# GEGLU feed-forward on one core: two feature tiles interleaved by product, and a head of two plain tiles with eight products taken ahead

## The chip, the cores and the metric

One core of one Trainium2 chip runs the whole program. The metric is the device time of one execution in microseconds (us), as a median of several executions. The profile shows one execution of each kernel; its span (first to last instruction) is about 1.8 us shorter than the device time of that execution.

Names used below: PE is TensorE (its matmuls), PEld its weight loads, DVE is VectorE, ACT is ScalarE, POOL is GpSimd, SP is the sync engine, which does nothing here but issue loads. "SPq" and "ACTq" are issues of loads on these two engines' queues. A load is issued at one time and "lands" when all its data is there. SBUF is the on-chip memory that tiles lie in, PSUM the banks that matmuls write to. KB is 1024 bytes. bf16 and fp32r are the 16-bit and the 32-bit float type of the matmuls here.

## The reference

```python
B, S, D, F = 32, 32, 1024, 3584        # bf16; x is 1024 x 1024 when flattened
def reference(x, w_gate, w_up, w_down):
    return (gelu(x @ w_gate) * (x @ w_up)) @ w_down
```

## The kernel before

The hidden layer has F/128 = 28 feature tiles. Four of them (the "head") are computed plainly: gate and up, for two token halves of 512, eight matmuls each. The other 24 tiles use a scheme with seven block products instead of eight (Strassen's, in Winograd's form): gate and up are two of the four blocks of one operand, the token halves the other. Five of the seven products are in fp32r, because their operands are sums; two are in bf16, because their operands are the inputs themselves. The down projection uses the same seven products once, on large blocks.

The head, cut to what matters (`plain` issues matmuls of a plain tile, `nb` is the token half):

```python
F0 = 4                                             # plain tiles
for q in range(1, 4):                              # loads: three more quarters of D
    load_xT(0, d0, d1)                             # x, transposed by the load, 256 KB
    load_w(nc.sync, 0, 0, d0, d1)                  # gate weights of the 4 tiles, 256 KB
    load_w(nc.sync, 0, 1, d0, d1)                  # up weights, 256 KB
load_xT(1, 0, KD); load_xT(1, KD, DT)              # second token half
...
for q in range(3):
    for which in (0, 1):                           # gate, up
        for dt in range(q * KQ, (q + 1) * KQ):
            for fl in range(F0):
                plain(head[fl][which], which, fl, 0, dt, dt + 1)
```

The loop takes one tile at a time. In it `prod` is four matmuls of 128x512:

```python
for ft in range(F0, FT):
    prod(psc, s1, t1, True)                 # fp32r
    sn5 = snap(psc, "sn5", 2)               # ACT copies PSUM to SBUF
    prod(psa, s2, t2, False)                # fp32r
    sn2 = snap(psa, "sn2", 1)
    if open_ft: last_product(open_ft)       # fp32r, of the tile before
    prod(psc, s4, b22r, False)              # fp32r
    c12 = added(sn2, psc)                   # DVE
    h1 = acc("G")                           # the gelu's result goes to a PSUM bank
    nc.scalar.activation(h1, c12, ACT.Gelu_apprx_tanh)
    prod(psb, quads(ci, fl)[1], b21, True)  # bf16: product P2
    ...
    ahead = first_product(ft + 1)           # bf16: product P1 of the next tile
    prod(psa, s3, t3, False)                # fp32r
    c22 = added(sn5, psa)
    tt(g_of(ft)[:, NB:], c22, h1, MUL)      # DVE
```

POOL makes the four weight sums s1 to s4 of the next two tiles meanwhile. PE's eight PSUM banks go by tags: A three, B two, C two, G one.

## Time and profile before

| | before |
|---|---|
| device time, median (3 runs at first) | 277.25 us |
| span of the profile | 275.2 us |
| PE busy | 270.1 us, 98% of the span |
| matmuls of 512 columns in the program | 432 bf16, 760 fp32r |

These lines are from the page of before: the span, then busy tenths in 40 equal slices (9 is 90% or more), PEclk is the granted clock of TensorE, and last the shares of the chain that ended last.

```profile
span 275.2 us, 3268 instructions
...
PE   8999999999999999999999999999999999999995
...
PEclk9999999999999999999999999999999999999999
...
PE 98%; issue 0%; ACT 0%
```

PE is full in every slice but the first and the last and makes up the whole chain: only fewer or cheaper matmuls, or fewer gaps between them, can shorten this kernel. The next lines are the timeline of PE for one tile of the loop (start in us, length in us, then line, tile written, tiles read, shapes, count).

```profile
56.21 1.03 PE L268 MATMUL psA<-b,wg 128*128 128x512 bf16 x4
56.88 1.27 PE L268 MATMUL psA<-t,s 128*128 128x512 f32 x4
...
60.72 1.07 PE L268 MATMUL psC<-b22r,s 128*128 128x512 f32 x4
61.86 0.81 PE L268 MATMUL psB<-b,wg 128*128 128x512 bf16 x3
62.51 0.38 PE L268 MATMUL psA<-b,wg 128*128 128x512 bf16 x1
```

From the start of one tile's P1 (56.21) to the next's (62.51) it is 6.30 us. The trace's start-to-start distances inside a run of equal matmuls are 216 ns for bf16 and 226 to 227 ns for fp32r. 8 x 216 + 20 x 226.7 ns are 6.26 us, so the two changes of type in each tile cost about 0.035 us together.

Of the head's loads, these are the three transposed ones of the first token half and the last up weights, as SP issues them (start, time that the issue takes):

```profile
1.74 1.33 SPq L189 DMA_TRANSPOSE b<-in_x_dram  x1
...
4.24 2.75 SPq L189 DMA_TRANSPOSE b<-in_x_dram  x1
...
8.18 1.27 SPq L189 DMA_TRANSPOSE b<-in_x_dram  x1
...
10.12 0.47 SPq L131 DMA_DIRECT2D wu<-in_w_up_dram  x1
```

PE's timeline from the first real matmul (4.38 us) to the start of the second token half (18.93 us):

```profile
4.38 1.39 PE L221 MATMUL psA<-b,wg 128*128 128x512 bf16 x3
...
6.48 0.38 PE L221 MATMUL psC<-b,wg 128*128 128x512 bf16 x1
6.84 0.60 PE L221 MATMUL psB<-b,wu 128*128 128x512 bf16 x2
...
15.91 0.59 PE L221 MATMUL psB<-b,wu 128*128 128x512 bf16 x2
...
18.93 1.89 PE L221 MATMUL psA<-b,wg 128*128 128x512 bf16 x8
```

In before, PE waits for loads only 0.14 us in this stretch (at the first up weights, 6.8 us). The last up weights of the first token half are issued at 10.12 us and land at 14.33 us.

### The profile page before, as it was taken

The numbers are of one execution on the slowest core, as the hardware profiler recorded it, in microseconds if no ns is written. First come the engines' busy times: TensorE is split into PE (matmuls) and PEld (weight loads), VectorE is DVE, ScalarE is ACT, GpSimd is POOL, SyncE is SP. The second block draws the span as 40 slices with busy tenths as digits, with TensorE's granted clock in tenths as the row PEclk, the third lists the DMA queues.
The fourth block names the chain that finished last, engine by engine and source line by source line (L and its number), as shares of the span: only waits on it lengthen the run. The fifth ranks groups of instructions, "written<-read, shape, count | busy, mean of one in ns | idle before, by whom it ended". The sixth has DMA issues, their size and how long they took to land.

```text
span 275.2 us, 3268 instructions
## 1 busy us (share of the span) xinstructions
PE 270.1 (98%) x1190; PEld 184.3 (67%) x1207; DVE 173.1 (63%) x184; ACT 114.4 (42%) x179; POOL 94.9 (34%) x51
## 2 busy tenths in 40 slices
PE   8999999999999999999999999999999999999995
PEld 3444467766677777777666777754447888888883
DVE  0049975555555555555555555556999999999511
ACT  4034455555555555555555555430200022972001
POOL 1000059996766749494947660000000000000000
PEclk9999999999999999999999999999999999999999
DMA  7999023150505143250508500003992245786202
GB/s 150 323 248 270 2 76 96 59 155 0 155 0 152 26 126 87 68 137 17 152 2 249 171 2 1 0 0 126 335 337 82 91 166 169 245 270 209 77 0 76
DMA packets 52192, 33.77 MB, mean 123 GB/s; under 512 B 8656, under 2 KB 52176, under 8 KB 52176
## 3 DMA queue, kind: packets, MB, share of 16 engines
q1 hardware_dynamic: 49184, 30.94, 39.1%
q10 hardware_dynamic: 2992, 2.62, 3.0%
q8 instruction: 9, 0.15, 0.2%
q14 instruction: 7, 0.06, 0.1%
HBM read 29.62 MB, written 2.10 MB: 115 GB/s over the span
## 4 chain that ended last, share of the span: by engine, by line
PE 98%; issue 0%; ACT 0%
PE psA L268 31%; PE psC L268 16%; PE psA L352 14%; PE psB L268 7%; PE psB L352 7%; PE psC L352 7%; PE psG L352 5%; PE psA L221 4%; PE psC L221 3%; PE psB L221 3%; PE psG L205 1%; PE psG L221 1%; PE tp L213 0%; ACT o_sb L491 0%; PE psG L217 0%
## 5 line engine op out<-in xcount | busy, mean ns | idle before, releaser
L268 PE MATMUL psA<-t,s 128*128 128x512 f32 x192 | 56.2, 414 | 0.0
L268 PEld LDWEIGHTS psA<-t,s 128*128 128x128 f32 x192 | 36.1, 188 | 9.4 <-ACT sn L279 0.2
L156 POOL TENSOR_TENSOR s<-wu 128x1024 fp32r<-128x1024 bf16 x11 | 23.7, 2150 | 29.3 <-PE psC L268 29.3
L284 DVE TENSOR_TENSOR c<-sn,psA 128x512 f32<-128x512 f32 x24 | 16.6, 690 | 25.4 <-PE psA L268 25.4
L268 PEld LDWEIGHTS <-wg 128*128 128x128 bf16 x192 | 16.9, 98 | 23.3 <-issue 6.3
L279 ACT COPY sn<-psA 128x512 f32<-128x512 f32 x48 | 27.8, 579 | 10.4 <-PE psA L268 10.4
L268 PE MATMUL psC<-t,s 128*128 128x512 f32 x96 | 26.1, 394 | 0.0
L268 PE MATMUL psA<-t,a22r 128*128 128x512 f32 x96 | 25.9, 391 | 0.0
L320 ACT ACTIVATE psG<-c 128x512 f32<-128x512 f32 x24 | 14.4, 602 | 27.4 <-DVE c L284 27.4
L268 PE MATMUL psC<-b22r,s 128*128 128x512 f32 x96 | 25.6, 389 | 0.0
L268 PE MATMUL psA<-b,wg 128*128 128x512 bf16 x96 | 24.6, 379 | 0.0
L158 POOL TENSOR_TENSOR s<-wg,s 128x1024 fp32r<-128x1024 bf16 x11 | 23.8, 2165 | 0.9
L157 POOL TENSOR_TENSOR s<-s,wg 128x1024 fp32r<-128x1024 f32 x11 | 23.5, 2137 | 0.9
L159 POOL TENSOR_TENSOR s<-wg,wu 128x1024 fp32r<-128x1024 bf16 x11 | 23.5, 2139 | 0.0
L268 PE MATMUL psB<-b,wg 128*128 128x512 bf16 x84 | 22.2, 381 | 0.8
L279 ACT COPY sn<-psC 128x512 f32<-128x512 f32 x24 | 14.1, 589 | 20.3 <-PE psC L268 20.3
L290 DVE TENSOR_TENSOR hi<-h,psA 128x512 bf16<-128x512 bf16 x14 | 9.6, 689 | 19.8 <-PE psA L268 19.8
L268 PEld LDWEIGHTS psC<-t,s 128*128 128x128 f32 x96 | 18.0, 188 | 4.3
L268 PEld LDWEIGHTS psA<-t,a22r 128*128 128x128 f32 x96 | 18.0, 188 | 3.8
L268 PEld LDWEIGHTS psC<-b22r,s 128*128 128x128 f32 x96 | 17.9, 188 | 3.8 <-ACT sn L279 0.2
L284 DVE TENSOR_TENSOR c<-sn,psC 128x512 f32<-128x512 f32 x24 | 16.5, 689 | 5.0 <-PE psC L268 5.0
L284 DVE TENSOR_TENSOR c<-sn,psB 128x512 f32<-128x512 f32 x24 | 16.5, 687 | 2.8
(99 smaller groups left out, 420.5 us busy)
## 6 DMA issues: line engine op xcount, KB each, us to landing
wg<-in_w_gate_dram SPq DMA_DIRECT2D x12, 512.0 KB, 4.0
wu<-in_w_up_dram SPq DMA_DIRECT2D x12, 512.0 KB, 5.2
wdb<-in_w_down_dram SPq DMA_DIRECT2D x12, 512.0 KB, 4.7
wdb<-in_w_down_dram SPq DMA_DIRECT2D x12, 384.0 KB, 4.2
v<-in_w_down_dram SPq DMA_DIRECT2D x4, 512.0 KB, 6.9
out_dram<-o_sb ACTq DMA_DIRECT2D x16, 128.0 KB, 1.7
v<-in_w_down_dram SPq DMA_DIRECT2D x4, 384.0 KB, 7.6
wg<-in_w_gate_dram SPq DMA_DIRECT2D x3, 256.0 KB, 3.9
```

What stands on the lines that cost most here:

```text
L156: yield eng.tensor_tensor(s1, a21, a22, ADD)
L157: yield eng.tensor_tensor(s2, s1, a11, SUB)
L158: yield eng.tensor_tensor(s4, a12, s2, SUB)
L159: yield eng.tensor_tensor(s3, a11, a21, SUB)
L205: nc.tensor.matmul(warm_ps, lhsT=ones_w, rhs=ones_m, start=True, stop=True)
L221: nc.tensor.matmul(ps, lhsT=w_tiles[0][which][:, dt, fl * P : (fl + 1) * P], rhs=x_rows(dt, nb), start=(dt == 0), stop=(dt == DT - 1),)
L268: nc.tensor.matmul(ps, lhsT=lhs[:, k, :], rhs=rhs[:, k, :], start=(start and k == 0), stop=(k == KD - 1), skip_group_check=True,)
L279: nc.scalar.copy(t, ps)
L284: tt(t, s, ps, ADD)
L290: tt(g_of(ft)[:, :NB], h0, psa, MUL)
L320: nc.scalar.activation(h1, c12, ACT.Gelu_apprx_tanh)
L352: nc.tensor.matmul(banks[m], lhsT=lhs(k)[:, m * P : (m + 1) * P], rhs=rhs(k), start=(start and k == 0), stop=(k == HF - 1), skip_group_che ...
```

## The change

The intent has three parts. First, 26 tiles instead of 24 in the form with seven products: 1184 matmuls instead of 1192. Secondly, the loop takes two tiles together and goes product by product, so that the four bf16 products of a pair stand in one block and the type changes half as often. Thirdly, the head with only two plain tiles has less work to cover its loads with, so the products P2 of the next eight tiles are computed in the head ("ahead") and kept in SBUF, in slots that later hold the hidden layer. The core of the diff:

```diff
-    F0 = 4
-    NCH = (FT - F0) // FC + 1
+    NCH = FT // FC
+    NAHEAD = 8
@@ banks
-        ... bufs={"A": 3, "B": 2, "C": 2, "G": 1}[tag]
+    BANKS = {"A": 4, "B": 2, "C": 2}
@@ loads of the head: the weight loads are half as large, and
+        load_ahead(0)                       # 512 KB for four ahead products
         load_xT(1, 0, KD)
         load_xT(1, KD, DT)
+        load_ahead(1)
@@ head
+        tok0 = [(acc("A"), acc("B")) for _ in range(FC)]
+        for q in range(3): ...              # as before, for two tiles
+        take_ahead(0, "CCAA", (nc.scalar.copy, nc.vector.tensor_copy) * 2)
+        ...                                 # second token half of the two tiles
+        take_ahead(1, "CCAA", (nc.scalar.copy,) * 4)
@@ loop
-        for ft in range(F0, FT):
+        for ci in range(1, NCH):
+            for fl in range(FC):
+                prod(psc[fl], s1[fl], t1, True)
+                sn5.append(snap(psc[fl], "sn5"))
+            for fl in range(FC):
+                prod(psa[fl], s2[fl], t2, False)
+                sn2.append(snap(psa[fl], "sn2"))
+            for st in open_fts:
+                last_product(st)
+            for fl, ft in enumerate(fts):
+                prod(psc[fl], s4[fl], b22r, False)
+                h1.append(gelu(added(sn2[fl], psc[fl]), "h1", 2))     # now in SBUF
+                a22r_of(ft)
+            if fts[0] < FC + NAHEAD:
+                h0 = first                                            # P2 was taken ahead
+            else:
+                ... # P2 of both tiles
+            begun = [first_product(ft + FC) for ft in fts]            # P1 of the next two
+            for fl, ft in enumerate(fts):
+                prod(psa[fl], s3[fl], t3, False)
+                tt(g_of(ft)[:, NB:], added(sn5[fl], psa[fl]), h1[fl], MUL)
```

The bank G is gone: the gelu result h1 goes to SBUF. The down projection does the same matmuls on renamed banks.

More of the change, by code (lines that the diff above doesn't have):

```diff
@@ L68 @@
     ring = ctx.enter_context(tc.tile_pool(name="ring", bufs=4))
-    opool = ctx.enter_context(tc.tile_pool(name="osb", bufs=4))
     one = ctx.enter_context(ExitStack())
@@ L101, in g_of @@
         return by_batch(g_lo if ft < HF else g_hi)(k)
+    BANKS = {"A": 4, "B": 2, "C": 2}
     def acc(tag):
-        return ps1.tile([P, NB], fp32, name=f"ps{tag}", tag=tag, bufs={"A": 3, "B": 2, "C": 2, "G": 1}[tag])
+        return ps1.tile([P, NB], fp32, name=f"ps{tag}", tag=tag, bufs=BANKS[tag])
+    a12_ahead = [ring.tile([P, KD, KB * P], bf16, name="a12a", tag="ring") for _ in range(NAHEAD // KB)]
     b11 = xpool.tile([P, KD, NB], bf16, name="b11")
@@ L114, in x_rows, with alloc_w, load_w_all @@
         return ((b11, b12), (b21, b22))[dt // KD][nb][:, dt % KD, :]
-    w_tiles = {
-        0: tuple(
-            gpool.tile([P, DT, F0 * P], bf16, name=n, tag=f"hi{KB}", bufs=2) for n in ("wg0", "wu0")
-        )
-    }
-    def alloc_w(ci):
-        w_tiles[ci] = tuple(
-            wpool.tile([P, DT, FC * P], bf16, name=n, tag=n, bufs=b) for n, b in (("wg", 3), ("wu", 2))
+    ahead = [
+        gpool.tile([P, KB, NB], fp32, name="ahead", tag=f"hi{KB}", bufs=2) for _ in range(NAHEAD // KB)
+    ]
+    w_tiles = {}
+    def alloc_w(ci, which):
+        w_tiles[ci, which] = wpool.tile(
+            [P, DT, FC * P], bf16, name=("wg", "wu")[which], tag=("wg", "wu")[which], bufs=(3, 2)[which]
         )
     def load_w(eng, ci, which, d0, d1):
-        f0, fc = (F0 + (ci - 1) * FC, FC) if ci else (0, F0)
+        f0 = ci * FC * P
         src = (wg_r, wu_r)[which]
-        eng.dma_start(out=w_tiles[ci][which][:, d0:d1, :], in_=src[:, d0:d1, f0 * P : (f0 + fc) * P])
-    def load_w_chunk(ci):
-        alloc_w(ci)
-        for which in (0, 1):
-            load_w(nc.sync, ci, which, 0, DT)
+        eng.dma_start(out=w_tiles[ci, which][:, d0:d1, :], in_=src[:, d0:d1, f0 : f0 + FC * P])
+    def load_w_all(ci, which):
+        alloc_w(ci, which)
+        load_w(nc.sync, ci, which, 0, DT)
     def quads(ci, fl=None):
         cols = slice(None) if fl is None else slice(fl * P, (fl + 1) * P)
-        wg, wu = w_tiles[ci]
+        wg, wu = w_tiles[ci, 0], w_tiles[ci, 1]
         return wg[:, :KD, cols], wg[:, KD:, cols], wu[:, :KD, cols], wu[:, KD:, cols]
-    def chunk_of(ft):
-        ci, fl = divmod(ft - F0, FC)
-        return ci + 1, fl
     s_tiles = {}
@@ L163, in a22r_of @@
     def a22r_of(ft):
-        t = spool.tile([P, KD, P], f32r, name="a22r", tag="a22r", bufs=3)
-        nc.scalar.copy(t, quads(*chunk_of(ft))[3])
+        t = spool.tile([P, KD, P], f32r, name="a22r", tag="a22r", bufs=2)
+        nc.scalar.copy(t, quads(*divmod(ft, FC))[3])
         a22rs[ft] = t
@@ L182 @@
             )
+        alloc_w(0, 0)
+        alloc_w(0, 1)
         for dt in range(KQ):
@@ L185, with load_ahead @@
         load_w(nc.scalar, 0, 1, 0, KQ)
+        def load_ahead(i):
+            f0 = (FC + i * KB) * P
+            nc.sync.dma_start(out=a12_ahead[i], in_=wg_r[:, KD:, f0 : f0 + KB * P])
         def load_xT(nb, d0, d1):
@@ L197 @@
             load_w(nc.sync, 0, 1, d0, d1)
+        load_ahead(0)
         load_xT(1, 0, KD)
         load_xT(1, KD, DT)
-        load_w_chunk(1)
-        load_w_chunk(2)
-        warm_ps = acc("G")
+        load_ahead(1)
+        load_w_all(1, 0)
+        load_w_all(1, 1)
+        load_w_all(2, 0)
+        warm_ps = acc("A")
         for _ in range(NWARM):
             nc.tensor.matmul(warm_ps, lhsT=ones_w, rhs=ones_m, start=True, stop=True)
-        tags = iter("CCAB")
+        tags = iter("CCBB")
         for dt in range(KQ):
@@ L210 @@
                 tag = next(tags)
-                tp = ps1.tile([P, hw], bf16, name="tp", tag=tag, bufs={"A": 3, "B": 2, "C": 2}[tag])
+                tp = ps1.tile([P, hw], bf16, name="tp", tag=tag, bufs=BANKS[tag])
                 for b in range(HALF):
@@ L222, in plain @@
                     ps,
-                    lhsT=w_tiles[0][which][:, dt, fl * P : (fl + 1) * P],
+                    lhsT=w_tiles[0, which][:, dt, fl * P : (fl + 1) * P],
                     rhs=x_rows(dt, nb),
@@ L227, in plain, with gelu @@
                 )
+        def gelu(src, tag, bufs):
+            h = ework.tile([P, NB], bf16, name=tag, tag=tag, bufs=bufs)
+            nc.scalar.activation(h, src, ACT.Gelu_apprx_tanh)
+            return h
         def plain_out(ft, nb, gate, up):
-            h = ework.tile([P, NB], bf16, name="h", tag="h")
-            nc.scalar.activation(h, gate, ACT.Gelu_apprx_tanh)
-            tt(g_of(ft)[:, nb * NB : (nb + 1) * NB], h, up, MUL)
-        head = [(acc(a), acc(b)) for a, b in ("AB", "AB", "AC", "CG")]
-        for q in range(3):
-            for which in (0, 1):
-                for dt in range(q * KQ, (q + 1) * KQ):
-                    for fl in range(F0):
-                        plain(head[fl][which], which, fl, 0, dt, dt + 1)
-        for fl in range(F0):
-            for which in (0, 1):
-                plain(head[fl][which], which, fl, 0, 3 * KQ, DT)
-            plain_out(fl, 0, *head[fl])
-        chunk1 = sums(1, nc.vector)
-        tt(t1, b12, b11, SUB)
-        after = (
-            lambda: (next(chunk1), tt(t2, b22, t1, SUB)),
-            lambda: (next(chunk1), next(chunk1)),
-            lambda: (tt(t3, b22, b12, SUB), a22r_of(F0)),
-            lambda: (next(chunk1), a22r_of(F0 + 1)),
-        )
-        for fl, (a, b) in enumerate(("AB", "AB", "AC", "AC")):
-            ps = acc(a), acc(b)
-            for which in (0, 1):
-                plain(ps[which], which, fl, 1, 0, DT)
-            if fl == 1:
-                nc.scalar.copy(b22r, b22)
-            plain_out(fl, 1, *ps)
-            after[fl]()
-        tt(t4, b21, t2, SUB)
-        g_hi = g_tiles("hi", bf16, N)
-        nc.gpsimd.tensor_copy(ident[:, :1], t4[:, 0, :1])
+            tt(g_of(ft)[:, nb * NB : (nb + 1) * NB], gelu(gate, "h0", 4), up, MUL)
         def prod(ps, lhs, rhs, start):
@@ L275, in prod, with ahead_of, take_ahead @@
                 )
-        def snap(ps, tag, bufs):
-            t = ework.tile([P, NB], fp32, name=tag, tag=tag, bufs=bufs)
-            nc.scalar.copy(t, ps)
-            return t
+        def ahead_of(ft):
+            i, j = divmod(ft - FC, KB)
+            return ahead[i][:, j, :]
+        def take_ahead(i, tags, engines):
+            for j, (tag, copy) in enumerate(zip(tags, engines)):
+                ps = acc(tag)
+                prod(ps, a12_ahead[i][:, :, j * P : (j + 1) * P], b21, True)
+                copy(ahead[i][:, j, :], ps)
+        tok0 = [(acc("A"), acc("B")) for _ in range(FC)]
+        for q in range(3):
+            for which in (0, 1):
+                for dt in range(q * KQ, (q + 1) * KQ):
+                    for fl in range(FC):
+                        plain(tok0[fl][which], which, fl, 0, dt, dt + 1)
+        for fl in range(FC):
+            for which in (0, 1):
+                plain(tok0[fl][which], which, fl, 0, 3 * KQ, DT)
+            plain_out(fl, 0, *tok0[fl])
+        take_ahead(0, "CCAA", (nc.scalar.copy, nc.vector.tensor_copy) * 2)
+        tt(t1, b12, b11, SUB)
+        tok1 = [(acc("A"), acc("B")) for _ in range(FC)]
+        for fl in range(FC):
+            for which in (0, 1):
+                plain(tok1[fl][which], which, fl, 1, 0, KD)
+        tt(t2, b22, t1, SUB)
+        nc.scalar.copy(b22r, b22)
+        for fl in range(FC):
+            for which in (0, 1):
+                plain(tok1[fl][which], which, fl, 1, KD, DT)
+            if fl == 0:
+                tt(t3, b22, b12, SUB)
+            plain_out(fl, 1, *tok1[fl])
+        load_w_all(2, 1)
+        take_ahead(1, "CCAA", (nc.scalar.copy,) * 4)
+        chunk1 = sums(1, nc.vector)
+        for _ in range(3):
+            next(chunk1)
         def added(s, ps):
@@ L285, in added, with snap, first_product @@
             return t
+        def snap(ps, tag):
+            t = ework.tile([P, NB], fp32, name=tag, tag=tag, bufs=2)
+            nc.scalar.copy(t, ps)
+            return t
+        def first_product(ft):
+            psa = acc("A")
+            prod(psa, quads(*divmod(ft, FC))[0], b11, True)
+            if ft < FC + NAHEAD:
+                return psa, gelu(added(ahead_of(ft), psa), "h0", 4)
+            return psa, snap(psa, "sn1")
         def last_product(st):
@@ L290, in last_product @@
             tt(g_of(ft)[:, :NB], h0, psa, MUL)
-        def first_product(ft):
-            psa = acc("A")
-            prod(psa, quads(*chunk_of(ft))[0], b11, True)
-            return psa, snap(psa, "sn1", 2)
-        open_ft = None
-        ahead = first_product(F0)
-        for ft in range(F0, FT):
-            ci, fl = chunk_of(ft)
-            fs = slice(fl * P, (fl + 1) * P)
-            if fl == 0:
-                nxt = sums(ci + 1, nc.gpsimd) if ci + 1 < NCH else iter(())
-                if ci + 2 < NCH:
-                    load_w_chunk(ci + 2)
-            s1, s2, s3, s4 = (s[:, :, fs] for s in s_tiles[ci])
-            (psa, sn1), psc, psb = ahead, acc("C"), acc("B")
-            prod(psc, s1, t1, True)
-            sn5 = snap(psc, "sn5", 2)
-            next(nxt, None)
-            prod(psa, s2, t2, False)
-            sn2 = snap(psa, "sn2", 1)
-            if ft + FC < FT:
-                a22r_of(ft + FC)
-            if open_ft:
-                last_product(open_ft)
-            prod(psc, s4, b22r, False)
-            c12 = added(sn2, psc)
-            h1 = acc("G")
-            nc.scalar.activation(h1, c12, ACT.Gelu_apprx_tanh)
-            prod(psb, quads(ci, fl)[1], b21, True)
-            c11 = added(sn1, psb)
-            h0 = ework.tile([P, NB], bf16, name="h", tag="h")
-            nc.scalar.activation(h0, c11, ACT.Gelu_apprx_tanh)
-            next(nxt, None)
-            if ft + 1 < FT:
-                ahead = first_product(ft + 1)
-            prod(psa, s3, t3, False)
-            c22 = added(sn5, psa)
-            tt(g_of(ft)[:, NB:], c22, h1, MUL)
-            open_ft = (ft, psa, h0)
@@ new lines @@
+        begun = [first_product(FC + fl) for fl in range(FC)]
+        next(chunk1, None)
+        tt(t4, b21, t2, SUB)
+        nc.gpsimd.tensor_copy(ident[:, :1], t4[:, 0, :1])
+        open_fts = []
+        for ci in range(1, NCH):
+            fts = range(ci * FC, (ci + 1) * FC)
+            if fts[0] == HF:
+                g_hi = g_tiles("hi", bf16, N)
+            if ci + 1 < NCH:
+                if ci + 2 < NCH:
+                    load_w_all(ci + 2, 0)
+                for _ in sums(ci + 1, nc.gpsimd):
+                    pass
+            s1, s2, s3, s4 = ([s[:, :, fl * P : (fl + 1) * P] for fl in range(FC)] for s in s_tiles[ci])
+            sn5, sn2, h1, h0 = [], [], [], []
+            psa, first = zip(*begun)
+            psc = [acc("C") for _ in fts]
+            for fl in range(FC):
+                prod(psc[fl], s1[fl], t1, True)
+                sn5.append(snap(psc[fl], "sn5"))
+            for fl in range(FC):
+                prod(psa[fl], s2[fl], t2, False)
[6 more added lines that the diff above has]
+                a22r_of(ft)
+            if ci + 2 < NCH:
+                load_w_all(ci + 2, 1)
+            if fts[0] < FC + NAHEAD:
+                h0 = first
+            else:
+                for fl in range(FC):
+                    psb = acc("B")
+                    prod(psb, quads(ci, fl)[1], b21, True)
+                    h0.append(gelu(added(first[fl], psb), "h0", 4))
+            begun = [first_product(ft + FC) for ft in fts] if ci + 1 < NCH else []
+            for fl, ft in enumerate(fts):
+                prod(psa[fl], s3[fl], t3, False)
+                tt(g_of(ft)[:, NB:], added(sn5[fl], psa[fl]), h1[fl], MUL)
+            open_fts = list(zip(fts, psa, h0))
@@ L375 @@
         p2_b21 = by_batch([load_b(LO, 0, b) for b in range(NBT)])
-        bankb = [acc(t) for t in "BCBC"]
+        bankb = [acc(t) for t in "CCBB"]
         span(bankb, by_batch(A12), p2_b21, 0, KB, False, True)
-        last_product(open_ft)
+        for st in open_fts:
+            last_product(st)
         span(bankb, by_batch(A12), p2_b21, KB, HF)
@@ L398, in store @@
         def store(m, tok, col, in0, in1):
-            o = opool.tile([P, NB], bf16, name="o_sb", tag="o_sb")
+            o = late.tile([P, NB], bf16, name="o_sb", tag="o_sb", bufs=MT)
             tt(o, in0, in1, ADD)
@@ L416 @@
         sb = snaps(bankb, "snb")
-        banka = [acc(t) for t in "AAAG"]
+        banka = [acc("A") for _ in range(MT)]
         product(banka, by_batch(A11), by_batch(v11), True)
@@ L488 @@
         for m in range(MT):
-            o = opool.tile([P, NB], bf16, name="o_sb", tag="o_sb")
+            o = late.tile([P, NB], bf16, name="o_sb", tag="o_sb", bufs=MT)
             r0 = NB + m * P
```

## The prediction

> **What bounds it now.** TensorE throughout: the page's chain that ended last is 98% PE, PE busy 270.1 of 275.2 us. Start-to-start distances in the trace: a 128x512 bf16 matmul takes 216 ns (the Trainium skill, "TensorE: Matmul & The Clock Gate", section "Wait — 56ns, not 53.3ns?", states 215.7 for this; it agrees), an fp32r one about 227 ns. 432 bf16 and 760 fp32r matmuls make 93.3 + 172.3 = 265.6 us; the rest is 4.4 us before the first real matmul, about 0.65 us at the half clock (to 5.6 us), about 3.5 us after the last matmul, and small gaps. One product-form tile lasts 6.30 us (timeline) against 8 x 216 + 20 x 226.7 = 6.26: about 0.035 us per round trip bf16 to fp32r and back. DVE, ACT and POOL are off the chain. In the head, loads run at 290-350 KB/us from 7.7 to 28 us, and the up weights of the fourth quarter land at 14.3 us, 0.9 us before PE reaches them.
>
> **What the change does.**
> 1. Two tiles move from plain form (32 bf16) to product form (8 bf16 + 20 fp32r): -48 bf16, +40 fp32r matmuls: -10.4 + 9.1 = -1.3 us, all on the chain.
> 2. Interleaving two tiles: about 13 switch round trips instead of 24: -0.4 us, on the chain.
> 3. Slack in the loop doubles, but PE waits for nothing there already: 0. POOL's four sums (8.6 us) still fit a pair of 12.5 us, or 10.8 us where P2 was taken ahead.
> 4. ACT loses eight snaps and DVE does the add instead: off the chain.
> 5. Head: the first token half now has 32 matmuls (6.9 us), so PE would be ready for the ahead block at about 12.0 us without waits. Loads needed by then: the same transposed x, half the weights in 512-byte pieces (128 KB in about 0.44 us), then 512 KB for the ahead block. From the landings before: 14.3 - 2.2 (768 KB less) + 0.4 (smaller pieces) + 1.5 (512 KB) - up to 0.5 (earlier first quarter) = about 13.8 us. So PE waits about 1.8 us in total at the second to fourth quarter and at the first ahead block, against 0.15 us now: +1.7 us. After that the second x half lands before its use, and t1, t2, three sums and the added pair finish on DVE about 1 us before PE needs them.
> 6. Down projection, last store: unchanged matmuls; only banks and pools are renamed: 0.
>
> **Sum.** 277.25 - 1.3 - 0.4 + 1.7 = 277.3. The landing estimate is the loosest term, rather high. I say 277.0 us, 8 in 10 within 275.7 to 278.3. Faster by over 2%: 0.01; within 2%: 0.96; slower by over 2%: 0.03.
>
> **What would show it.** 1184 real matmuls, 800 of them fp32r; a pair at about 12.56 us in the timeline (12.60 before for two); PE idle of 1 to 2.5 us between 6.5 and 14 us, put down to DMA; no PE waits from 14 us on; the down projection lasts as before.
>
> **What would make it wrong.** Landings earlier than I think (down to 275.5); DVE late for the first sums or adds near 31 us, or POOL's sums late for the second pair; idle in the head long enough that the clock falls back to half (the same page, "Why this matters for your kernels", warns of gaps over about 3 us): then several us slower.

## The result, and the profile after

| | before | after |
|---|---|---|
| median of the timed runs (6 and 6) | 277.12 us | 277.72 us |
| lowest to highest | 276.86 to 277.41 | 277.15 to 278.38 |
| ratio after to before, 95% interval | | 1.0022, 1.0004 to 1.004 |
| the changed kernel again, with other runs of before (6 and 11) | 277.01 us | 277.19 us, ratio 1.0015, 1.0001 to 1.003 |
| span of the profile | 275.2 us | 275.3 us |
| first product of the loop starts | 33.42 us | 29.09 us |
| first matmul of the down projection | 183.14 us | 182.15 us |

A ratio is the mean time of one kernel's runs over the mean of the other's of the same rounds, so it is not quite the ratio of the medians. The change is within 2%, and slower by some 0.2%. The profile after happens to be of the fastest of its six runs.

From the page of after, the lines that answer to those shown of before, with the second line of the chain (its shares by line):

```profile
span 275.3 us, 3334 instructions
...
PE   8899999999999999999999999999999999999994
...
PEclk9999999999999999999999999999999999999999
...
PE 93%; SPq 3%; DMA 2%; issue 1%; ACT 0%
PE psA L245 35%; PE psC L245 18%; PE psA L382 18%; PE psC L382 7%; PE psB L382 7%; PE psB L245 5%; DMA a12a<-in_w_gate_dram 2%; SPq L192 1%; SPq L133 1%; PE psA L227 1%; PE psB L227 1%; ACT o_sb L522 0%; SPq L176 0%
```

The chain is no longer all PE: 3% of it is SP issuing loads, and 2% the landing of the load "a12a", the weights of the first ahead block. The chain in order of time shows where that lies (start, length, what):

```profile
1.74 1.33 SPq L192
...
4.24 1.45 SPq L192
...
6.88 1.23 SPq L192
...
8.15 0.58 SPq L133
...
9.29 4.39 DMA a12a<-in_w_gate_dram
...
13.72 0.61 PE psC L245 x2
```

Up to 9.29 us the chain runs through the loads that SP issues one after the other; then the load of a12a is awaited for 4.39 us, and only from 13.72 us on is it PE. In PE's timeline of the same stretch the last bracket is the idle time before the group and what ended it:

```profile
4.50 1.02 PE L227 MATMUL psA<-b,wg 128*128 128x512 bf16 x4
5.54 1.04 PE L227 MATMUL psB<-b,wu 128*128 128x512 bf16 x4
6.97 1.04 PE L227 MATMUL psA<-b,wg 128*128 128x512 bf16 x4 [0.40 <-DMA wg<-in_w_gate_dram]
...
8.90 1.04 PE L227 MATMUL psA<-b,wg 128*128 128x512 bf16 x4
...
11.59 0.60 PE L227 MATMUL psA<-b,wg 128*128 128x512 bf16 x2 [0.80 <-DMA wg<-in_w_gate_dram]
...
13.72 1.90 PE L245 MATMUL psC<-b,a12a 128*128 128x512 bf16 x7 [0.23 <-DMA a12a<-in_w_gate_dram]
```

A group of four takes 0.86 us at 216 ns each, and what a group's start lies later than that is waiting, also where no bracket is shown (a matmul's modelled length of 0.38 us covers part of a gap). From the start of the first real matmul (4.50 us) to that of the ahead block (13.72 us) there are 9.22 us for 32 matmuls, which need 32 x 0.216 = 6.91: TensorE stands for 2.31 us. In before the comparable loss in the head is about 0.7 us (14.55 us for 64 matmuls), 0.14 of it waiting for loads and the rest matmuls at half the clock in the first 1.2 us. In this profile of after there are none at half the clock: the first distances are 215 ns.

The loop itself is as intended. These are the lines for one pair, P1 to P1:

```profile
92.39 1.89 PE L245 MATMUL psA<-b,wg 128*128 128x512 bf16 x8
93.92 2.19 PE L245 MATMUL psA<-t,s 128*128 128x512 f32 x8
...
101.39 1.97 PE L245 MATMUL psC<-b22r,s 128*128 128x512 f32 x8
103.43 1.67 PE L245 MATMUL psB<-b,wg 128*128 128x512 bf16 x7
104.94 0.38 PE L245 MATMUL psA<-b,wg 128*128 128x512 bf16 x1
```

92.39 to 104.94 us are 12.55 us for two tiles (12.60 before), with P2 (psB) and P1 (psA) of both tiles in one bf16 block.

So the sum by the two traces, after less before: -1.3 us of matmuls (counted: 48 bf16 less, 40 fp32r more), about -0.5 us of type changes (24 ways there and back become 13; in the first experiment below, with 12, the last matmul ends 0.53 us earlier than in before), 2.31 - 0.7 = +1.6 us in the head, and +0.1 us because the first real matmul starts at 4.50 instead of 4.38 us: -0.1 us, as the ends of PE's work show (271.84 against 271.94 us). The spans differ by +0.18 us all the same, since from the end of PE's work to the end of the span it is 3.50 us in after and 3.22 us in before (3.21 to 3.50 us in all the traces). The timed runs say +0.2 to +0.6 us, and the two profiled runs themselves took 277.15 and 276.96 us.

### The profile page after: what moved, and what is told of

It reads as the page before. It is cut to its first block, busy times and chain, and to the rows that moved or that the text cites. A ratio compares the mean times of both kernels' runs of the same rounds, so it can differ in the third digit from the quotient of the medians.

```text
span 275.3 us, 3334 instructions
## 1 busy us (share of the span) xinstructions
PE 268.6 (98%) x1183; PEld 187.6 (68%) x1199; DVE 194.1 (70%) x192; ACT 113.1 (41%) x185; POOL 107.9 (39%) x55
## 4 chain that ended last, share of the span: by engine, by line
PE 93%; SPq 3%; DMA 2%; issue 1%; ACT 0%
PE psA L245 35%; PE psC L245 18%; PE psA L382 18%; PE psC L382 7%; PE psB L382 7%; PE psB L245 5%; DMA a12a<-in_w_gate_dram 2%; SPq L192 1%; SPq L133 1%; PE psA L227 1%; PE psB L227 1%; ACT o_sb L522 0%; SPq L176 0%
## 5 line engine op out<-in xcount | busy, mean ns | idle before, releaser
L245 PE MATMUL psA<-t,s 128*128 128x512 f32 x208 | 54.1, 402 | 0.0
L237 ACT ACTIVATE h<-c 128x512 bf16<-128x512 f32 x52 | 31.9, 629 | 37.9 <-DVE c L297 37.9
L245 PEld LDWEIGHTS psA<-t,s 128*128 128x128 f32 x208 | 39.1, 188 | 9.2
L153 POOL TENSOR_TENSOR s<-wu 128x1024 fp32r<-128x1024 bf16 x12 | 26.6, 2217 | 26.3 <-PE psC L245 14.1
L154 POOL TENSOR_TENSOR s<-s,wg 128x1024 fp32r<-128x1024 f32 x12 | 27.7, 2312 | 0.9
L302 ACT COPY sn<-psA 128x512 f32<-128x512 f32 x44 | 24.8, 584 | 7.5 <-PE psA L245 7.2
L156 POOL TENSOR_TENSOR s<-wg,wu 128x1024 fp32r<-128x1024 bf16 x12 | 27.1, 2258 | 0.0
L155 POOL TENSOR_TENSOR s<-wg,s 128x1024 fp32r<-128x1024 bf16 x12 | 26.3, 2190 | 0.9
L361 DVE TENSOR_TENSOR lo<-c,h 128x512 bf16<-128x512 f32 x12 | 18.1, 1508 | 0.6
L425 ACT COPY snb<-psC 128x512 f32<-128x512 f32 x4 | 2.1, 589 | 36.5 <-PE psC L382 36.5
```

Source lines behind the costliest of these rows:

```text
L153: yield eng.tensor_tensor(s1, a21, a22, ADD)
L154: yield eng.tensor_tensor(s2, s1, a11, SUB)
L155: yield eng.tensor_tensor(s4, a12, s2, SUB)
L156: yield eng.tensor_tensor(s3, a11, a21, SUB)
L237: nc.scalar.activation(h, src, ACT.Gelu_apprx_tanh)
L245: nc.tensor.matmul(ps, lhsT=lhs[:, k, :], rhs=rhs[:, k, :], start=(start and k == 0), stop=(k == KD - 1), skip_group_check=True,)
```

## The experiments

The theory (in the expectations: theory H) was that the whole loss against the arithmetic lies in the head, as waits for loads. The rival (theory L) was the loop: DVE's product into the hidden layer got slower there. These are the groups of that operation, of before, of after, and of the first experiment (the last but one number of a line is the mean in ns):

```profile
L331 DVE TENSOR_TENSOR lo<-c,psG 128x512 bf16<-128x512 f32 x10 | 6.9, 689 | 1.5 <-DVE c L284 0.5
```

```profile
L361 DVE TENSOR_TENSOR lo<-c,h 128x512 bf16<-128x512 f32 x12 | 18.1, 1508 | 0.6
```

```profile
L338 DVE TENSOR_TENSOR lo<-c,h 128x512 bf16<-128x512 f32 x10 | 15.1, 1505 | 0.3
```

With h1 in PSUM it took 689 ns, with h1 in SBUF 1508 ns on the mean, from 692 to 2624 ns. The Trainium skill, "SBUF — State Buffer", section "SBUF: two separate sides", says that a VectorE operation with two SBUF inputs and a GpSimd operation that reads SBUF take one port pair as an exclusive lock, held for a whole instruction. The traces agree: h1's move to SBUF gave the operation its second SBUF input, POOL's sums got longer too (means of 2.14 to 2.17 us before, 2.19 to 2.31 us after), and the shortest of the slow group takes what all took before. The single operations of after show the lock: of 26, the 12 slow ones each ran beside a sum of POOL and ended 0.55 us after that sum ended; the other 14 took 691 to 693 ns, and all but one of these had no sum beside them. In before the operation took 686 to 690 ns beside POOL too.

All runs in one table. "Ahead block" is the start of the first ahead product in the trace, "loop" the time from the first product of the loop to the down projection. Each ratio is to runs of before on the same chip in the same rounds, 5 rounds each.

| run | median us | ratio to before, 95% interval | ahead block | loop | span |
|---|---|---|---|---|---|
| after, again | 277.19 | 1.0015 (1.0001 to 1.003) | 13.77 | 153.07 | 275.4 |
| pairs with the head of before | 276.46 | 0.9984 (0.9973 to 0.9996) | none | 147.42 | 274.6 |
| the same again | 276.51 | 0.9984 (0.9968 to 1.0) | none | 147.42 | 274.8 |
| no weight loads in quarters 2 to 4 (wrong result) | 275.75 | 0.9955 (0.9943 to 0.9967) | 12.03 | 153.07 | 273.5 |
| half the bytes in them (wrong result) | 277.15 | 1.0008 (0.9991 to 1.0024) | 13.90 | 153.06 | 275.5 |
| half as many of them (wrong result) | 276.58 | 0.9983 (0.9967 to 0.9999) | 13.55 | 153.04 | 275.0 |
| four of them merged into two | 277.45 | 1.0021 (1.0004 to 1.0039) | 14.33 | 153.07 | 275.8 |
| ACT issues four, late | 282.66 | 1.0202 (1.0178 to 1.0225) | 20.06 | 153.07 | 282.0 |
| ACT issues three, reordered | 283.07 | 1.0225 (1.0197 to 1.0254) | 18.08 | 153.07 | 279.7 |
| POOL issues four | 278.89 | 1.0074 (1.0037 to 1.0111) | 15.45 | 153.06 | 276.9 |
| ACT issues two, first | 277.42 | 1.0023 (1.0007 to 1.0038) | 14.21 | 153.05 | 275.8 |
| P1 of the first pair early | 278.50 | 1.0055 (1.0039 to 1.007) | 15.85 | 153.68 | 277.1 |

In after itself the loop lasted 153.06 us. The loop of every variant with the changed kernel's loop order in the head is the same to 0.03 us, and the span less the start of the ahead block is 261.4 to 261.6 us in all of them (two rows are outside: in the ACT row with 20.06 the clock was still low when the block started, and the last row has another head). What these kernels differ in, they differ in before the ahead block.

### The changed kernel again

No edit. 

> The changed kernel once more, for its spread and a second trace. Theory H (the head): the loss against the arithmetic (-1.7 us) is the wait of TensorE for loads in the first token half; this trace again shows 2 to 3.3 us of distance above 216 ns between matmuls before 14 us, the runs lie at 277.1 to 278.4, and their spread (1.2 us against 0.6 us before) comes from there. Theory L (the loop): the longer VectorE products (1.5 us mean against 0.69) and slower GpSimd sums cost time in the loop; then the pairs of tiles between 90 and 180 us take more than 12.6 us.

Measured: the same pattern in the second trace. The ahead block starts at 13.77 us, and the head loses 2.36 us, now with some matmuls at half the clock (the first four take 1.11 us instead of 0.86); the pairs between 90 and 180 us take 12.56 us. The spread was no evidence: before, with eleven runs, went from 276.32 to 277.33 us, nearly as wide as after (276.94 to 278.10).

### Pairs with the head of before

```diff
 # before's head of four plain tiles and its loads; bank G renamed to a fourth A
-        for ft in range(F0, FT): ...     # one tile at a time, h1 in PSUM
+        for ci in range(1, NCH): ...     # the changed kernel's loop of pairs, h1 in SBUF,
+                                         # no product ahead, 12 pairs
```

> The head of before (four plain tiles, no product ahead) with the new interleaved loop of pairs, 12 pairs instead of 24 single tiles; the same matmuls as before (432 bf16, 760 fp32r). Theory H: only the saved switches show: 12 x 0.035 = 0.4 us less than before, about 276.7; the VectorE products are as slow as in the changed kernel and cost nothing. Theory L: the slow VectorE products cost what they cost in the changed kernel: 277.5 or more.

Measured: 276.46 us, and 276.51 us in a second set, 0.16% below before in both (the second interval just reaches 1.0). Its span is 0.4 to 0.6 us shorter. Theory H had said 0.4. DVE's product is as slow as in after (1505 ns), with no cost. Theory L falls: it would have made this run slower than before. This version is correct, has the changed kernel's loop and is the fastest correct one here, by 0.2% against before and 0.3% against after (1.0015 in the same rounds).

> The pairs with the head of before once more, beside the other: 276.3 to 276.7, ratio to before 0.997 to 0.9995.

### No weight loads in three quarters

```diff
         for q in range(1, 4):
             load_xT(0, d0, d1)
-            load_w(nc.sync, 0, 0, d0, d1)
-            load_w(nc.sync, 0, 1, d0, d1)
@@ plain
-                    lhsT=w_tiles[0, which][:, dt, ...]
+                    lhsT=w_tiles[0, which][:, dt % KQ, ...]      # wrong result on purpose
```

> Wrong result on purpose: the plain tiles use the weights of the first quarter in all quarters, and the six weight loads of the other quarters (768 KB, 3.1 us of issue) are left out. Theory H: TensorE waits at most 0.6 us in the first token half, 275.5 to 276.3. Theory L: 277.3 or more, as the loop is untouched.

Measured: 275.75 us, ratio 0.9955. PE waits for no load from 4.5 us on; what is left in its head are three matmuls at the half clock (0.6 us):

```profile
4.48 1.67 PE L225 MATMUL psA<-b,wg 128*128 128x512 bf16 x4
...
12.03 1.89 PE L243 MATMUL psC<-b,a12a 128*128 128x512 bf16 x8
```

The ahead block starts 1.69 us earlier than in after, and the span is 1.8 us shorter. This is what the changed kernel would be worth if its head's loads were free: -1.25 us by the timed runs (0.0045 x 277), -1.7 us by the spans, against -1.7 us by the arithmetic.

### Half the bytes, and half the number of loads

Which property of those loads costs? One run halves their size and keeps their number; one halves their number and so also the bytes. Their outputs are wrong, which doesn't matter for the times.

```diff
 # half the bytes
-            load_w(nc.sync, 0, 0, d0, d1)
-            load_w(nc.sync, 0, 1, d0, d1)
+            load_w(nc.sync, 0, 0, d0, d0 + 1)
+            load_w(nc.sync, 0, 1, d0, d0 + 1)
 # half the number
-            load_w(nc.sync, 0, 0, d0, d1)
-            load_w(nc.sync, 0, 1, d0, d1)
+            load_w(nc.sync, 0, 0, d0, d1)       # up uses the gate weights from here on
```

> Wrong result on purpose: the changed kernel with as many loads in the head, but each of the six weight loads of quarters two to four brings one of its two rows of blocks (64 KB instead of 128 KB; 384 KB less in all). If bytes bind between 7 and 14 us: at some 250 KB/us the ahead block lands 1.5 us earlier and the time falls to about 275.9. If the issuing on the sync queue binds: the ahead block lands at most 0.4 us earlier, 276.8 or more.

> Wrong result on purpose: the up half of the plain tiles uses the gate weights from the second quarter on, so three of the six weight loads are left out. As many bytes less (384 KB) as in the run with half the bytes, which gained 0.2 us at most, but three issues less (some 1.4 us). If the number of loads on the one queue is what delays the ahead block: it lands at 12.2 to 12.8 us instead of 13.7, and the time is 275.8 to 276.5. If neither counts and the transposes of x alone set the pace: 276.8 to 277.3.

Measured: with half the bytes nothing is gained (277.15 us, ahead block at 13.90 us; the last weights land 0.7 us earlier, at 11.2 us, but the ahead block's load does not). With half the number 276.58 us, ratio 0.9983 against 1.0008, two intervals that overlap only between 0.9991 and 0.9999. In its trace the ahead block's load was issued 1.35 us earlier than in after (7.94 against 9.29 us) but landed only 0.4 us earlier (13.26 against 13.68), not the 0.9 us or more that was expected. PE waited 1.3 us in one piece, now for the gate weights of the fourth quarter: the first of the 16 parts of that load landed at 10.14 us, the last at 11.77. So halving the bytes of the weight loads gains nothing that shows; halving their number too may gain something like half a microsecond, but the intervals overlap; and the two together do not explain when the loads land. Lines of SP for the half-bytes run show the issue times that stayed:

```profile
5.51 0.58 SPq L133 DMA_DIRECT2D wg<-in_w_gate_dram  x1
6.13 0.43 SPq L133 DMA_DIRECT2D wu<-in_w_up_dram  x1
6.61 1.23 SPq L192 DMA_TRANSPOSE b<-in_x_dram  x1
...
8.98 0.43 SPq L188 DMA_DIRECT2D a12a<-in_w_gate_dram  x1
```

Each of these loads of 64 KB occupies SP for 0.43 to 0.58 us, as long as one of 128 KB did. "DMA: Bandwidth & Descriptors" of the Trainium skill, in "Rules for kernel authors", advises to coalesce small transfers and says that under 64 KB one pays mostly overhead. The issue times agree so far: they hardly fall from 128 KB to 64 KB. Smaller loads were not run.

### Two loads merged

```diff
+        load_xT(0, KQ, 2 * KQ);       load_w(..., 0, KQ, 2 * KQ);  load_w(..., 1, KQ, 2 * KQ)
+        load_xT(0, 2 * KQ, 3 * KQ);   load_w(..., 0, 2 * KQ, DT);  load_w(..., 1, 2 * KQ, DT)
+        load_xT(0, 3 * KQ, DT);       load_ahead(0)
```

> The changed kernel with the weights of the third and fourth quarter brought by one load per matrix (same bytes, two issues less, some 1.05 us), and the fourth x quarter after them. If issuing binds: the ahead block lands about 1 us earlier, 276.0 to 276.6. If bytes bind: 277.0 to 277.4. No cold clock either way.

Measured: 277.45 us, no gain. SP had two issues less, but its last transposed x load took 2.62 us to issue instead of 1.23, so the ahead block's load was issued at 9.74 us, later than in after; and the merged gate weights landed at 10.4 us, for which PE waited 1.6 us at the third quarter. An issue on SP is thus not a fixed cost: the same kind of load took 1.23 us to issue in one kernel and 2.62 us in another. What it stands for was not tested.

### Issuing from another engine

Four tries to take issues off SP.

```diff
 # first try (ACT, late): weights of quarters 3 and 4 issued by ACT after its two copies
+        for q in (2, 3):
+            for which in (0, 1):
+                load_w(nc.scalar, 0, which, q * KQ, (q + 1) * KQ)
 # second try (ACT, reordered): three of them, other loads moved behind them in the program
 # third try: the same four issued by POOL (nc.gpsimd)
 # fourth try (ACT, first): instead, the two loads of the second quarter, before ACT's copies
```

> The changed kernel, but the four weight loads of the third and fourth quarter are issued by ScalarE after its two copies (from about 4.8 us), so that the sync queue has four issues (2.1 us) less before the ahead block's load. Theory H in the form that issuing binds (in the changed kernel's chain of waits the sync queue's issues fill 0.7 to 9.8 us): the ahead block lands 1 to 2 us earlier, TensorE waits 0.5 to 1.3 us instead of 2.3, and the time is 276.0 to 276.9. If the bytes bind (DMA engines busy), nothing changes: 277.4 to 278.0.

> Second try at issuing from ScalarE. In the first try its loads stood until 7.1 us waiting for earlier loads that had used the same semaphores (a load waited for its semaphore's former load to land). Here three of the loads (both of the third quarter, gate of the fourth) stand in the program where those semaphores' loads have landed by 4 to 5.4 us. If that was the fault: issues at 4.7 to 6.3 us, the ahead block issued near 7.5 us, 275.7 to 276.6, no cold clock. If loads on ScalarE's queue are slow beside a full sync queue whatever their issue: they land 3 us or more after issue, and the time is 277 to 280.

> As the first try, but the four loads of the third and fourth quarter are issued by GpSimd, which is idle in the head, so that a wait for a semaphore stops no copy. If issuing binds and GpSimd issues in good time: 275.8 to 276.8. If its issue is late or its loads slow: slower than the changed kernel, as the first try was (281 to 284), with a low clock in the trace.

> Correct version: ScalarE issues the two loads of the second quarter before its copies (2.3 to 3.3 us; they use semaphores that no load has used before, so nothing to wait for). The sync queue has two issues (1.05 us) less ahead of everything later; ScalarE's copies come 0.5 us later, which the wait for the second quarter hides. If the number of loads on the sync queue delays the ahead block: about 1 us earlier, 276.1 to 276.8. If loads on ScalarE's queue are slow beside the transposes, as in the tries before (4 us and more from issue to landing): they land at 7.5 us or later and the time is 277.5 to 279.

Measured: none gained; the first and second lost over 5 us against the changed kernel. The profile of the second is of its fastest run (281.47 us), the only one with the full clock; the other five, 282.96 to 284.64 us, had a mean clock of 0.986 to 0.988. In the first try ACT's four issues began at 7.10, 7.59, 8.31 and 9.38 us, though ACT was free from 4.7 us; the loads that had used the same semaphores before landed at 7.08, 7.47, 8.29 and 9.35 us. The second try was meant to avoid that and failed to: its issues began at 7.08, 8.45 and 9.46 us, again just after landings on the same semaphores (7.06, 8.43, 9.44). So it did not test what it was made for. Once issued, these loads of 128 KB needed 4 to 8 us to land. In the fourth try nothing held up the first issue (2.27 us), yet that load landed at 7.75 us, and the second, issued at 3.49 us (0.02 us after a landing on its semaphore), at 9.84 us. ACT's copies came later for it, and the first real matmul started at 5.63 us. In the third try POOL's issues were early (1.29 to 3.93 us), but these loads needed 4.8 to 6.9 us to land, a12a was issued only at 10.49 us, behind two transposed loads whose issue took 6.18 us together, and the six runs spread from 276.72 to 280.45 us.

So in these tries loads of ACT and POOL landed late beside SP's transposed loads, whatever their issue. But SP's own were late as well: in the fourth try its first two transposed loads landed at 8.05 and 10.09 us, against 6.46 and 8.16 in the changed kernel. Loads that stood in one queue in front of a12a and of x's second half now ran beside them: in the first try a12a, issued at 7.22 us, landed at 13.40 us, before ACT's second load (issued at 7.59, landed at 13.74). Whether that is the whole reason was not tested. The Trainium skill, "DMA: Bandwidth & Descriptors", section "Issuing engines are not separate DMA queues", says that a second issuing engine saves only the sequencer's time; these runs agree, and even that saving was lost.

The first try shows a second cost. Windows of its trace (busy us of each engine, then the granted clock, the DMA share and GB/s):

```profile
12.00:14.00 2.00, 0.60 (x3) 0.11 (x2) 0.00 (x0) 0.00 (x0) 0.00 (x0) 0.97 1.19 140
14.00:16.00 2.00, 1.63 (x4) 0.29 (x2) 0.00 (x0) 0.00 (x0) 0.00 (x0) 0.50 1.31 204
...
20.00:22.00 2.00, 2.00 (x9) 0.88 (x8) 0.69 (x1) 0.60 (x2) 0.00 (x0) 0.83 1.09 342
```

After waits of 2.33 and 1.40 us, with four matmuls between them, the clock fell to half at 13.9 us and stayed there until 20.7 us. The prediction had named this slowdown as a risk. In the changed kernel the waits are 0.2 to 1.0 us each and the clock stays full.

### Filling the wait

```diff
+            if q == 1:                    # after the second quarter
+                for ft in range(FC, 2 * FC):      # P1 of the first pair: needs b11 only
+                    psa = acc("A"); prod(psa, quads(...)[0], b11, True); early.append(psa)
 # loads: the upper half of that pair's gate weights moved in front of the third quarter
 # DVE: the adds of the first pair before the sums, t3 after them; POOL waits for t3, not t4
```

> Correct version, to fill the wait instead of shortening the loads: the first products of the first pair (8 bf16 matmuls, 1.73 us, they need only the first half of x and 256 KB of weights that are loaded anyway) go between the second and third quarter of the first token half; VectorE's order in the head is adapted, GpSimd starts one sum earlier. If TensorE's wait in the head is what is lost and nothing else: the wait before the ahead block falls from 2.3 to about 1.2 us and the time from 277.2 to about 276.2 to 276.8. If the later loads only come later by the 256 KB: 277.0 to 277.5. VectorE late for the first sums would show as waits near 29 us.

Measured: 278.50 us, worse than after. PE was indeed fed until 14.2 us but for short waits, with the third quarter free of them, but the ahead block's load, now one issue later, landed 3.0 us after the load before it, at 15.80 us:

```profile
8.70 1.89 PE L248 MATMUL psA<-b,wg 128*128 128x512 bf16 x8
...
13.75 0.59 PE L230 MATMUL psB<-b,wu 128*128 128x512 bf16 x2
15.85 1.90 PE L248 MATMUL psC<-b,a12a 128*128 128x512 bf16 x8 [1.50 <-DMA a12a<-in_w_gate_dram]
...
27.12 1.24 PE L248 MATMUL psC<-b,a12a 128*128 128x512 bf16 x5 [0.74 <-ACT h L240]
```

The new order of banks added a wait for ACT (0.9 us before 27.12), and the new order on DVE and POOL another 0.6 us in the first pairs: POOL's first sum now ran beside DVE's sum t4 and took 4.21 us instead of 2.14, and PE waited for POOL's first two sums. So the idea of filling the wait was not refuted; this arrangement of it lost.

### What stays open

What sets the landings in the head. The ahead block's load of 512 KB needed 4.4 us from the start of its issue in after, 4.9 us with half the bytes ahead of it, 5.3 us with half the loads ahead of it and 6.0 us with one more. Neither halving the bytes nor issuing it 1.35 us earlier moved the start of the ahead block by more than 0.2 us; of all the runs only the one without the six weight loads brought it forward by more. In every one of these kernels the two transposed loads of the second half of x are issued directly behind it. Whether they hold it up was not tried.

The single packets in the traces narrow it. In the run that filled the wait, 90% of the load's 512 packets of 1 KB had started by 13.83 us, but the last 31 started one after the other, about 42 ns apart, from 14.11 to 15.38 us. In after half had started by 12.09 us and the last one at 13.23; in the fourth try of another engine, without such a tail, the packets started between 11.76 and 13.32 us. So in the slow cases a last small part sets the landing. 512 packets on 16 DMA engines are 32 each, so it looks like one engine that came late (an inference: the packets do not name their engine). What made it late is not shown.

## Why the prediction was right

The measured 277.72 us (and 277.19 us) lies in the range of 275.7 to 278.3, within 2%, as forecast. Point by point:

1. Fewer matmuls, -1.3 us: right. The counts are as predicted, the distances of 216 and 227 ns held (216 ns also agrees with the 215.7 ns of the Trainium skill's "TensorE: Matmul & The Clock Gate", section "Wait — 56ns, not 53.3ns?"), and the run without weight loads shows what is left when the head does not wait.
2. Fewer type changes, -0.4 us: right. A pair takes 12.55 us against 12.60, and pairs alone gain 0.16% or 0.45 us, twice.
3. No gain and no loss in the loop: right in the time, incomplete in the account. The prediction took POOL's sums at 8.6 us and DVE's products as they were, and did not see that h1's move to SBUF would make them block each other. The slack was enough: 153.06 us in every variant.
4. ACT and DVE off the chain: right, although DVE's busy time grew from 173.1 to 194.1 us.
5. The head, +1.7 us: right in size. Waits of 2.31 us against a loss of 0.7 us make +1.6; the ahead block was expected at about 13.8 us and started at 13.72. Right for partly wrong reasons: the sum was made of bytes (768 KB less, 512 KB more, smaller pieces), and the run with 384 KB less showed no gain from fewer bytes. That the terms added up is in part luck. The account was also wrong on the half clock, which it left as it was (PE ready at 12.0 us; without slow matmuls it is 4.50 + 6.91 = 11.41): in before it costs about 0.6 us; in after's profile there is none, and in its second trace, which has some, the head loses 2.36 instead of 2.31 us, since PE waits for the second quarter anyway. Two readings of the trace of before were off too, without effect on the sum: PE reaches the last up weights 1.6 us after they land, not 0.9, and the rate of 290 to 350 KB/us held only to 13 us (229 to 274 from 13 to 20 us).
6. Down projection: right; from its first matmul to the start of its last it is 89.3 us after and 88.4 before, the 0.9 us being one last product more (four fp32r matmuls of 227 ns) that now falls behind that mark.

The step that was off is the last one. The terms sum to 277.3, and the prediction shaded that to 277.0 because it held the landing estimate to be "rather high". Nothing in the trace of before said so, and the landing came within 0.1 us of the estimate. The unshaded sum is nearer to both medians, 277.72 and 277.19 us.

## What to carry to other kernels

Work that is removed from the start of a kernel has also been covering that start's loads: before cutting it, compare PE's arrival at each tile with the landing of its data in the old trace, and count the difference as a cost of the change. Here 1.7 us of saved PE time were paid back by 1.6 us more lost in the head, and the half of the change that leaves the head alone (pairs with the old head, 276.5 us) was the better kernel. When loads bind, find out by halving bytes and halving number separately which of them does, before moving issues to another engine; here neither answered it alone.

## What the Trainium skill lacked or had wrong

- "TensorE: Matmul & The Clock Gate", section "Why this matters for your kernels", warns of idle gaps over about 3 us. In the first ACT try the clock fell after gaps of 2.33 and 1.40 us with about 1 us of work between them, so shorter gaps close together can be enough; in the second ACT try gaps of 2.07, 1.43 and 1.77 us did not bring it down in the profiled run (mean clock 1.0), while the other five runs of that kernel had a mean clock of 0.986 to 0.988. A single limit on one gap does not describe this.
- "DMA: Bandwidth & Descriptors", section "Issuing engines are not separate DMA queues", calls the time to initiate a load usually small beside the load itself. Here, in after, it was 0.47 to 0.58 us of 3.0 to 3.8 us from issue to landing for a load of 128 KB, but 1.23 to 1.45 us of 3.6 to 4.7 us for a transposed one of 256 KB (2.75 us in before), one after the other on SP, and the issues up to 9.3 us stand in the chain of waits.
- No page read here says how late a load can land that ACT or POOL issues beside transposed loads of SP: 4 to 8 us for 128 KB from ACT in three kernels, 4.8 to 6.9 us from POOL in one, against 3.0 to 3.8 us from SP in after.
- No page read here gives the cost of changing between bf16 and fp32r matmuls: about 0.035 us for the way there and back by the sum of a tile (0.04 by the pairs: 12.60 against 12.56 us), beside 227 against 216 ns per matmul of 512 columns.
